# A transformer block on one core: W2 in 512 columns, the second norm by tile, and a new order of the instructions

## The chip, the core and the metric

The kernel runs on one NeuronCore of a Trainium2 chip. Its engines run side by side and meet through semaphores: TensorE (PE; its weight loads are shown as PEld), VectorE (DVE), ScalarE (ACT), GpSimd (POOL) and SyncE (SP), which here issues nearly all DMAs. The metric is device time in microseconds (us), the median of several executions; lower is better.

## What is computed

A block with adaptive layer norm: attention with 32 query heads and one shared key and value head, and a gated FFN. The input x has 2048 tokens of 1024 channels, all in bfloat16.

```
mod = silu(c) @ w_mod, split into sa, ca, ga, sb, cb, gb     (1024 each)
h = layernorm(x) * (1 + ca) + sa
q = h @ wq (32 heads of 32);  k = h @ wk;  v = h @ wv       (one head of 32)
x = x + ga * (concat_heads(softmax(q k^T / sqrt(32)) v) @ wo)
h = layernorm(x) * (1 + cb) + sb
out = x + gb * ((silu(h @ w1) * (h @ w3)) @ w2)             (F = 3584)
```

## The kernel before

**Tiling.** `build` cuts the tokens into 8 blocks n of 256 tokens, each of two tiles t of 128. An attention unit u = 8n + f is one block and four heads. A unit has 8 cycles; one cycle (`s_exp`) is 8 score matmuls of 32 rows (four at a time side by side in the array) into PSUM, and two exponentials of 128x1024 on ScalarE into one of 10 buffers U. That is 512 cycles and 1024 exponentials. Scores rotate through six PSUM banks (S); everything else on TensorE shares two banks (PB) until the last exponential has been done, and then has all eight.

**After a unit's exponentials** (`av`): VectorE adds pairs of U into PS (`pairs`) and folds these further, to 4 terms in units 2 to 7, to 1 term from unit 8 on (`level`); the denominators (`dens`) multiply the terms that are left with ones; `av_mm` makes the product with V (64 matmuls of 32 columns). In `attend` VectorE transposes the denominators, takes reciprocals, transposes back and scales, which puts the unit's output into QT. Units 0 and 1 are done together in `two_units`.

**After a block's 8 units** (`wo`): 32 matmuls of 512 columns with wo (already scaled by ga) in four sums of 8, each added to x; `ln_stats` (two BATCH_NORM_STATS2, the aggregate, then on Pool the addition of epsilon and the power −0.5) and `ln_norm` on VectorE, tile by tile. The normalised tile must be transposed for the FFN. In blocks 0 and 7, 16 PE transposes go into two banks, one for each half of the channels and each with both tiles, and VectorE applies (1 + cb) and sb out of PSUM in 8 instructions of 256 columns. In blocks 1 to 6 each tile goes through a DMA transpose into the freed part of QT, and VectorE applies the modulation there, in 8 instructions.

**FFN.** `ffn1` has 14 slabs of 256 FFN channels: 16 matmuls of 256 columns with w1, 16 with w3, a tanh on ScalarE and two VectorE instructions, which give HHT. A slab's weights (`slab_dma`, 2 x 512 KB) go into one of three buffers W13. `ffn2` has four quarters of 256 output columns (`quarter`): 28 matmuls of 256 columns for each tile, both tiles in one bank; `result` multiplies by gb and adds to x. A quarter's W2 (1792 KB) goes into one of two buffers W2S; in block 7 the last two quarters use the freed QT and U. Block n's FFN runs on TensorE during block n+1's attention. Block 7's FFN has no attention beside it.

**Order.** Every operation is a node with an engine, reads, writes, a duration and a due time (`vt`). `Placer` simulates the engines and, at each step, takes the ready node with the least due time, plus an offset for its tag and engine that `PLAN` gives. PLAN has one entry for every 8 score steps: slacks, flags and changed offsets. The engines' instruction streams are then fixed in this order. `Placer` knows a cost for each switch of TensorE between kinds of matmul (SWITCH): scores (S), AV and denominators (A), whole-array (F). Projections can also run in column form (C), in which one matmul is cut into four of 32 columns, and which needs no switch after A. `mode_of` allows column form for at most 12 operations in a row and while a running fetch load stays under FULL. Mod chunks (`mod_chunk`) compute the other parts of `mod` during block 0's attention.

All operations are emitted through `play`, so that all rows of the profile have the line 22. Rows are told apart by their tiles: `S<-QT,KT` scores, `U<-S` exponentials, `PB<-U,V` AV, `<-PS,ONES` denominators, `<-WO,QT` wo, `<-IDENT,XNB` transposes, `<-QT,W` or `<-HT,W` slabs and query projections (W is W13, whose space held wq before; the third slab buffer lies in HT, as do HHT, H20, TS and O2B), `<-W2S,HT` W2.

Of the kernel before, what the change touches and what calls it, by code (L numbers as in the profile page):

```python
# [8 lines left out]
P = 128  # L9
# [33 lines left out]
class Graph:  # L43
# [64 lines left out]
    def alias(self, new, old):  # L108
# [8 lines left out]
    (0, 0.08, 0.11, 0, 1.1, {"an/dve": 11, "av/dve": 9, "d0/sp": -38, "d1/sp": 10, "d11/sp": 2, "d12/sp": -4,  # L117
     "d2/sp": 51, "d3/sp": -151, "d6/sp": 67, "d7/sp": 32, "d8/sp": -29, "ev/act": -21, "k/pe": -26, "k/dve": 40,
     "ln/pe": -51, "ln/act": 32, "ln/dve": -11, "ln/pool": 57, "mc/pe": 52, "mc/sp": -2, "mod/pe": -62,
     "mod/dve": 10, "nm/act": 79, "pair/dve": -129, "q/pe": 3, "q/dve": -57, "quarter/pe": 11, "quarter/dve": -2,  # L120
     "s/pe": 67, "s/act": -3, "slab/pe": -5, "slab/act": 81, "slab/dve": 30, "v/pe": -8, "wo/pe": -78, "wo/dve": 1,
     "wo/sp": 36}),
    (0, 0.36, 0.11, 1, 1, {"an/dve": 8, "av/pe": -111, "av/dve": 2, "d0/sp": -31, "d1/sp": 16, "d10/sp": -66,
     "d12/sp": 63, "d13/sp": -1, "d3/sp": -14, "d5/sp": 2, "d7/sp": 84, "d8/sp": -2, "ev/act": -29, "k/pe": -36,
     "k/dve": -9, "kb/pe": 72, "ln/dve": 124, "mod/dve": -5, "nm/act": 32, "pair/dve": -104, "quarter/dve": 2,
     "s/pe": 55, "s/act": 107, "slab/pe": -26, "slab/act": -5, "slab/dve": 33, "slab/sp": 94, "v/dve": -118,
     "v/pool": -34, "wo/pe": -76, "wo/dve": 4, "wo/pool": -59, "wo/sp": 21, "d11/sp": 0, "d2/sp": 0, "d6/sp": 0,
     "ln/pe": 0, "ln/act": 0, "ln/pool": 0, "mc/pe": 0, "mc/sp": 0, "mod/pe": 0, "q/pe": 0, "q/dve": 0,
     "quarter/pe": 0, "v/pe": 0}),
    (0, 0.14, 0.18, 2, 2.9, {"q/dve": -32, "wo/dve": -44, "slab/act": 0}),  # L130
    (0.06, 0.11, 0.27, 0, 3.9, {"av/dve": 9, "d0/sp": -58, "d1/sp": 20, "d10/sp": 257, "d13/sp": 2, "d2/sp": 3,
     "d3/sp": -2, "d4/sp": 1, "d8/sp": 83, "ev/act": -11, "k/pe": -49, "k/dve": 1, "kb/dve": -7, "ln/pe": -5,
     "mc/pe": 63, "mc/sp": 5, "nm/act": 30, "out/sp": 1, "s/act": 114, "slab/sp": 4, "v/dve": 3, "v/pool": -26,
     "wo/pe": -78, "wo/dve": 14, "wo/pool": -23, "an/dve": 0, "d12/sp": 0, "d7/sp": 0, "ln/dve": 0, "mod/dve": 0,
     "pair/dve": 0, "q/dve": 0, "quarter/dve": 0, "s/pe": 0, "slab/pe": 0, "slab/dve": 0, "wo/sp": 0, "av/pe": 0,
     "d5/sp": 0, "kb/pe": 0}),
    (0, 0.11, 0.05, 0, 0.6, {"d6/sp": 19, "ev/act": -9, "k/pe": -81, "wo/pool": 7, "s/act": 0}),
    (0, 0.11, 0.05, 0, 0.6, {}),
    (0.13, 0.12, 0.23, 0, 0.7, {"av/pe": -5, "d0/sp": -4, "d10/sp": -68, "d3/sp": -46, "d9/sp": 72, "ev/act": -16,
     "kb/pe": 2, "ln/dve": -11, "mc/pe": -7, "mod/dve": -3, "q/dve": -85, "q/sp": -6, "quarter/pe": 4,  # L140
     "slab/act": 82, "slab/dve": 33, "slab/sp": 16, "wo/pe": -5, "wo/dve": 3, "wo/pool": 15, "av/dve": 0,
     "d1/sp": 0, "d2/sp": 0, "d6/sp": 0, "k/pe": 0, "k/dve": 0, "ln/pe": 0, "mc/sp": 0, "nm/act": 0, "d13/sp": 0,
     "v/dve": 0, "v/pool": 0, "d4/sp": 0, "kb/dve": 0, "out/sp": 0}),
    (0.24, 0.09, 0.2, 1, 1.4, {"av/pe": -4, "d7/sp": 78, "ev/act": -13, "ln/pool": -2, "mod/pe": 5,
     "pair/dve": -16, "slab/act": 83, "d0/sp": 0, "mod/dve": 0}),
    (0.24, 0.09, 0.02, 1, 0.4, {"d2/sp": -4}),
# [1220 lines left out]
```

## Time and profile before

| | |
|---|---|
| median of 3 runs | 1139.53 us (1138.42 to 1140.11) |
| the profiled execution | 1139.48 us |
| its span, first to last instruction | 1137.5 us |
| mean granted TensorE clock | 0.992 |
| PE / PEld busy | 1102.1 / 752.4 us |
| DVE / ACT / POOL busy | 989.8 / 1020.1 / 39.1 us |
| DMA | 209.64 MB, mean 184 GB/s |

Times in the profile count from the start of the span. A timeline row has start, length, engine, line, operation, what it writes and reads, shapes and the number of merged instructions; in brackets stands the idle time of the engine before it and what ended that. A row of a group has the busy time and the mean length in ns of one instruction, then the idle time before them and its releasers. The length of a matmul includes its way through the array; matmuls overlap, so that what one costs is the distance of their starts. "issue" as a releaser means that the engine waited for nothing that the profile shows. The granted clock is the share of full speed that TensorE got.

### The profile page before, as it was taken

Reading aid. Unit: us, or ns where it says so; the run is one execution under the profiler, and the core shown is the slowest. Engines: PE = TensorE matmul, PEld = TensorE weight load, DVE = VectorE, ACT = ScalarE, POOL = GpSimd, SP = SyncE. Lnnn points to the kernel's source line nnn. Section 1 sums busy time; section 2 is a strip of 40 time slices with the busy share of each in tenths; the row PEclk is TensorE's granted clock in tenths of the full one; section 3 lists DMA queues with packets and bytes.
Section 4 is the critical chain, followed back from the end, with each engine's and each line's share of the span. In section 5 each row is a group of like instructions: output and inputs, shape, how many; then the busy total and the mean of one; then the engine's idle time right before and its main releaser. Section 6 shows DMA issues by size and latency. Waiting matters only on the chain.

```text
span 1137.5 us, 37371 instructions
## 1 busy us (share of the span) xinstructions
PE 1102.1 (97%) x16835; PEld 752.4 (66%) x16860; DVE 989.8 (87%) x1617; ACT 1020.1 (90%) x1159; POOL 39.1 (3%) x91
## 2 busy tenths in 40 slices
PE   5999998999899999999999999999999999999998
PEld 4744536766467766777577766776567757776887
DVE  7998999999989989998999899998989899997442
ACT  5999999999999999999999999999989999994110
POOL 5200000000000000000000000000000000000000
PEclk9999989999999999999999999999999999999999
DMA  9320586675756666865596577868686558767993
GB/s 347 104 76 22 166 217 187 193 205 139 168 150 194 190 176 160 240 190 151 137 287 192 151 190 202 227 193 216 142 245 192 156 152 226 210 198 197 239 240 103
DMA packets 381535, 209.64 MB, mean 184 GB/s; under 512 B 17600, under 2 KB 373184, under 8 KB 381376
## 3 DMA queue, kind: packets, MB, share of 16 engines
q1 hardware_dynamic: 380944, 207.11, 65.9%
q8 instruction: 133, 2.18, 0.8%
q14 instruction: 26, 0.21, 0.1%
q10 hardware_dynamic: 432, 0.13, 0.0%
HBM read 199.89 MB, written 4.19 MB: 179 GB/s over the span
## 4 chain that ended last, share of the span: by engine, by line
PE 48%; ACT 42%; DVE 6%; DMA 1%; issue 1%; SPq 1%; POOL 0%; DVEq 0%
ACT U L22 39%; PE PB L22 34%; PE S L22 14%; ACT HT L22 3%; DVE PS L22 2%; DMA W<-in_A_wq_dram 1%; DVE ST L22 1%; SPq L22 1%; DVE X L22 1%; DVE RB L22 0%; DVE QT L22 0%; DVE HT L22 0%; DVE XNB L22 0%; DVE WO L22 0%; DVE MV L22 0%
## 5 line engine op out<-in xcount | busy, mean ns | idle before, releaser
L22 ACT ACTIVATE U<-S 128x1024 bf16<-128x1024 f32 x1024 | 966.6, 1142 | 11.5 <-PE S L22 10.7
L22 DVE TENSOR_TENSOR PS<-U 128x2048 bf16<-128x2048 bf16 x256 | 308.2, 1216 | 12.0 <-ACT U L22 10.1
L22 DVE TENSOR_TENSOR PS<-PS 128x1024 bf16<-128x1024 bf16 (+1 forms) x420 | 282.5, 689 | 2.5
L22 PE MATMUL PB<-QT,W 128*128 128x256 bf16 (+1 forms) x2688 | 228.1, 276 | 0.4 <-DVE HT L22 0.4
L22 PE MATMUL S<-QT,KT 32*128 32x256 bf16 x4096 | 204.7, 274 | 10.1 <-ACT U L22 7.8
L22 PEld LDWEIGHTS PB<-QT,W 128*128 128x128 bf16 (+1 forms) x2688 | 171.2, 98 | 42.0 <-issue 23.6
L22 PE MATMUL PB<-W2S,HT 128*128 128x256 bf16 x1512 | 189.3, 273 | 0.0
L22 PEld LDWEIGHTS PB<-W2S,HT 128*128 128x128 bf16 x1512 | 137.4, 98 | 41.5 <-issue 22.0
L22 PEld LDWEIGHTS S<-QT,KT 32*128 32x128 bf16 x4096 | 60.8, 92 | 139.5 <-ACT U L22 130.9
L22 PE MATMUL PB<-U,V 128*32 128x256 bf16 x4096 | 130.9, 276 | 3.5 <-issue 2.3
L22 PEld LDWEIGHTS PB<-U,V 128*32 128x32 bf16 x4096 | 101.8, 97 | 27.8 <-issue 15.3
L22 PE MATMUL PB<-QT,HT 128*128 128x256 bf16 (+1 forms) x1216 | 117.0, 273 | 0.0
L22 PE MATMUL PB<-HT,W 128*32 128x512 bf16 (+2 forms) x884 | 99.2, 343 | 3.1 <-DVE XNB L22 1.0
L22 PEld LDWEIGHTS PB<-QT,HT 128*128 128x128 bf16 (+1 forms) x1216 | 86.4, 97 | 21.0 <-issue 11.4
L22 ACT ACTIVATE HT<-PB 128x512 bf16<-128x512 f32 (+1 forms) x105 | 77.0, 733 | 7.9 <-PE PB L22 7.8
L22 DVE SCALAR_TENSOR_TENSOR HT<-HT,PB 128x512 bf16<-128x512 bf16 x100 | 68.3, 683 | 6.7 <-ACT HT L22 6.5
L22 PEld LDWEIGHTS PB<-HT,W 128*128 128x128 bf16 (+1 forms) x896 | 50.6, 97 | 34.3 <-issue 13.4
L22 DVE TENSOR_TENSOR HT<-HT,PB 128x512 bf16<-128x512 bf16 x100 | 68.2, 682 | 4.4 <-PE PB L22 3.1
L22 ACT ACTIVATE HT<-S 128x512 bf16<-128x512 f32 (+1 forms) x17 | 12.1, 721 | 58.9 <-PE S L22 58.9
L22 DVE STREAM_TRANSPOSE RB<-PB 128x256 f32<-128x256 f32 x63 | 28.0, 444 | 33.8 <-PE PB L22 33.4
L22 PE MATMUL PB<-WO,QT 128*128 128x512 bf16 (+1 forms) x260 | 53.2, 381 | 1.4 <-issue 0.6
L22 POOL TENSOR_SCALAR RS<-MV 128x1 f32<-128x1 f32 x32 | 10.2, 322 | 1009.3 <-DVE MV L22 1008.6
(111 smaller groups left out, 661.7 us busy)
## 6 DMA issues: line engine op xcount, KB each, us to landing
W<-in_B_w_dram SPq DMA_DIRECT2D x150, 512.0 KB, 4.6
W2S<-in_B_w_dram SPq DMA_DIRECT2D x30, 1792.0 KB, 8.5
HT<-in_B_w_dram SPq DMA_DIRECT2D x74, 512.0 KB, 4.7
W2S<-in_w_mod_dram SPq DMA_DIRECT2D x8, 1024.0 KB, 6.3
X<-in_A_x_dram SPq DMA_DIRECT2D x8, 512.0 KB, 7.2
U<-in_w_mod_dram SPq DMA_DIRECT2D x4, 1024.0 KB, 12.2
out_dram<-X SPq DMA_DIRECT2D x7, 512.0 KB, 7.7
W2S<-in_A_x_dram SPq DMA_DIRECT2D x5, 512.0 KB, 9.7
```

The lines of the kernel that those rows point to most:

```text
L22: return getattr(e, call[0])(*call[1], **call[2])
```

## The change

- **W2 of 512 columns.** `half` takes the place of `quarter`: two halves of 512 output columns, 28 matmuls of 512 columns for each tile, each tile in a bank of its own. A half's W2 comes in four transfers of 896 KB (7 of the 28 row blocks each) into four places. The second tile runs through the places backwards, and the next half's first part goes into the place that comes free first. In the last half of block 7, the second tile is cut into two times 256 columns.
- **Second norm by tile for blocks 0, 1 and 7.** One bank and 8 PE transposes for each tile, 16 modulations of 128 columns; block 1 no longer uses DMA transposes. In block 7 the second tile's 8 modulations run on ScalarE. In these blocks the epsilon is added on VectorE.
- **Last unit of blocks 0, 1 and 7** (`av_sharp`): the denominators take two folded terms of the first six cycles and the four half-buffers U of the last two cycles directly; AV of the first six cycles no longer waits for the last exponentials.
- **Order.** The fetch load is gone. `Placer.fetched` counts TensorE's instructions in blocks of 256 and models when a block has been fetched and when TensorE stops for one. The cap on column form by FULL goes; a switch from C to S costs 0.09 more, one from S 0.122 in place of 0.11. All of PLAN is new and longer.
- **Last block.** The sums with wo may take a bank before all that they read is ready (after the last exponential). Slabs 3 to 5 go into three places in the freed U.
- **Smaller ones.** The bias of query groups 2 to 7 is computed in four column groups at once (`q_bias_rest`); the scaled wq has keys of its own; the diagonal for the gate rows lies in W2's space and not in a norm buffer; mod chunks are due at 4 + 3i in place of 8 + 5i. `act_stats` is defined but used by no tile.

The core of the diff:

```diff
-    SWITCH = {"F": 0.095, "S": 0.11, "A": 0.106, "C": 0.106}
+    SWITCH = {"F": 0.095, "S": 0.122, "A": 0.106, "C": 0.106}
+    CS = 0.09
-    FULL = 36.0
-    FETCH = 24.0
+    BLOCK, AHEAD, STOP, CALL, MOST, LAND = 256, 141, 430, 0.6, 4.5, 2.6
...
-        return n.col[1][0] or ("C" if self.mode in ("A", "C") and self.ncol < self.COLS and self.load < self.FULL else "F")
+        return n.col[1][0] or ("C" if self.mode in ("A", "C") and self.ncol < self.COLS else "F")
...
+    def fetched(self, count):
+        self.pos += 2 * count
+        while self.pos >= self.BLOCK * len(self.fetch) + self.AHEAD:
+            self.fetch.append(min(max(self.t["pe"] + self.CALL, self.bw), self.t["pe"] + self.CALL + self.MOST) + self.LAND)
+        while self.pos >= self.BLOCK * self.got + self.STOP:
+            self.t["pe"] = max(self.t["pe"], self.fetch[self.got])
+            self.got += 1
...
+    def av_sharp(u):
+        s = Sess(False)
+        c0 = u * NJ
+        for q in range(0, NP - 2, 2):
+            pairs(c0 + q)
+        G.tag = "av"
+        fold(c0 + 2, 0, 2)
...
+        for q in range(NJ):
+            av_mm(u, c0 + q, q, s, q == 0, q == NJ - 1, [exps[(c0 + (5 if q < 6 else 7), 1)]])
+        sd = Sess()
+        terms = [("U", c0 + q, kk) for q in (6, 7) for kk in range(2)]
+        terms = [("PS", 0, 0), ("PS", 4, 0)] + terms
...
-                s = Sess()
+                s = Sess(n < NB - 1)
...
+                       after=[exps[(64 * NB - 1, 1)]] if n == NB - 1 else ())
...
-            if 0 < n < NB - 1:
+            if 1 < n < NB - 1:
...
-        for hh in range(2):
+        for t in range(2):
             s = Sess()
+            op("pe", lambda b, t=t: [lambda e, cc=cc: e.transpose(
+                BANKH[b][:, cc * P:(cc + 1) * P], XN[t][:, cc * P:(cc + 1) * P], IDENT[:]) for cc in range(NC)], 0.5,
+               reads=[("XN", t), "IDENT"], writes=[("h2", n, t)], vt=vt, mode="F", sess=s, post=0.145)
...
+    W13U = [Uf[:, (2 + k) * 4096:(3 + k) * 4096].rearrange("p (m c f) -> p m c f", m=2, c=NC) for k in range(3)]
...
+        if n == NB - 1 and 3 <= s < 6:
+            return W13U[s - 3], ("W13U", s - 3)
...
-    def quarter(n, q, vt):
+    def half(n, h, vt0, vt1):
         G.tag = "quarter"
+        for k in range(4):
+            w2_dma(n, h, k, vt0 + k - (200 if n == NB - 1 and h and k < 2 else 20))
+        ends = n == NB - 1 and h == 1
+        for t in range(2):
+            vt = vt0 + (vt1 - vt0) * t / 2
+            parts = [(0, 256), (256, 512)] if ends and t else [(0, 512)]
+            order = [(k, i) for k in (range(4) if t == 0 else range(3, -1, -1)) for i in range(NK)]
...
-        mod_chunk(i, 8.0 + 5 * i)
+        mod_chunk(i, 4.0 + 3 * i)
...
-            av(8 * n + f)
+            (av_sharp if f == NC - 1 and n in (0, 1, NB - 1) else av)(8 * n + f)
         e0 = 64.0 * (n + 1)
-        wo(n, e0 - 30)
+        wo(n, e0 - (330 if n == NB - 1 else 30))
```

568 lines of the change are left out of this document (347 added, 221 removed), and 10 rows, old and new, of the table PLAN.

## The prediction

> **What bounds the kernel now.** I read the page's chain first, then the busy times by stretch, then the timeline of the stretches in which TensorE stands idle.
>
> ```profile
> span 1137.5 us, 37371 instructions
> PE 48%; ACT 42%; DVE 6%; DMA 1%; issue 1%; SPq 1%; POOL 0%; DVEq 0%
> L22 ACT ACTIVATE U<-S 128x1024 bf16<-128x1024 f32 x1024 | 966.6, 1142 | 11.5 <-PE S L22 10.7
> ```
>
> The chain is shared by TensorE and ScalarE. ScalarE's 1024 exponentials take 966.6 us, and it stood idle for only 11.5 us ahead of them. The windows view (stretch; its length, then busy time of PE, PEld, DVE, ACT, POOL; clock; DMA share; GB/s) shows which of the two sets the end:
>
> ```profile
> 31.00:147.00 116.00, 112.82 (x2120) 60.72 (x2128) 107.11 (x187) 115.55 (x126) 7.24 (x17) 1.00 0.26 87
> 147.00:190.00 43.00, 37.96 (x567) 19.92 (x572) 39.09 (x70) 39.75 (x45) 2.44 (x4) 0.93 0.82 222
> 303.00:319.00 16.00, 10.13 (x171) 4.67 (x164) 14.05 (x29) 14.85 (x17) 0.79 (x2) 0.79 0.63 134
> 319.00:829.00 510.00, 507.66 (x7939) 349.50 (x7949) 470.18 (x746) 507.67 (x581) 7.43 (x16) 1.00 0.71 191
> 829.00:842.00 13.00, 10.48 (x220) 6.84 (x214) 9.37 (x15) 9.56 (x13) 0.00 (x0) 0.87 0.85 230
> 842.00:1038.00 196.00, 195.51 (x3037) 136.87 (x3032) 181.25 (x286) 194.78 (x224) 2.44 (x4) 1.00 0.68 187
> 1038.00:1060.50 22.50, 22.45 (x231) 16.70 (x230) 15.93 (x34) 0.05 (x1) 1.69 (x4) 1.00 0.95 244
> 1060.50:1135.00 74.50, 74.19 (x680) 66.24 (x678) 24.95 (x41) 8.36 (x14) 0.00 (x0) 1.00 0.75 199
> ```
>
> From 319 us on, TensorE works without a break to 1135 us, except for one hole at 829 to 842 us. Both engines are full in between, and after 1038 us (the last exponential) TensorE works alone. So the end is TensorE's work, plus the time it lost earlier. It lost time in three places: 147 to 190 (5.0 us idle and a clock of 0.93), 303 to 319 (5.9 us idle, clock 0.79) and 829 to 842 (2.5 us idle, clock 0.87). Time won there is work done before 1038 us that is not left over behind it. Idle time before 147 us doesn't count in the same way: ScalarE is full there, and TensorE has little else to do until block 0's attention is complete.
>
> **Part A, block 1's second norm by PE transposes.**
>
> ```profile
> 283.56 1.06 PE L22 MATMUL PB<-U,V 128*32 128x256 bf16 x32
> 308.58 0.55 DVE L22 TENSOR_SCALAR XNB<-X,MV,RS 128x1024 bf16<-128x1024 bf16 x1
> 308.81 0.40 PE L22 MATMUL S<-QT,KT 32*128 32x256 bf16 x8 [1.44 <-ACT U L22]
> 309.16 1.24 SPq L22 DMA_TRANSPOSE QT<-XNB  x1
> 311.55 1.90 PE L22 MATMUL PB<-U,V 128*32 128x256 bf16 x32 [0.30 <-ACT U L22]
> 313.93 1.90 PE L22 MATMUL PB<-U,V 128*32 128x256 bf16 x32
> 316.22 2.13 DVE L22 TENSOR_SCALAR QT<-QT,MODC 128x256 bf16<-128x256 bf16 x8
> 317.83 1.70 PE L22 MATMUL PB<-QT,HT 128*128 128x256 bf16 x14
> ```
>
> The second tile is normalised at 309.13. Its transpose goes through a DMA, the modulation follows at 316.22, and the first slab at 317.83, which is 8.7 us later. Meanwhile block 0's FFN has run out, and TensorE has only scores and AV, in the end at half speed (twice 32 AV matmuls in 1.90 us, against 1.06). After the change come 8 transposes for each tile and 16 modulations out of PSUM. Block 0 does this today in other sizes:
>
> ```profile
> 157.21 1.06 PE L22 MATMUL PB<-U,V 128*32 128x256 bf16 x32
> 159.60 0.80 PE L22 MATMUL PB<-PS,ONES 128*32 128x256 bf16 x16
> 174.01 0.55 DVE L22 TENSOR_SCALAR XNB<-X,MV,RS 128x1024 bf16<-128x1024 bf16 x1 [0.77 <-POOL RS L22]
> 174.61 1.07 PE L22 MATMUL PB<-IDENT,XNB 128*128 128x128 bf16 x16 [0.47 <-DVE XNB L22]
> 175.40 2.64 DVE L22 TENSOR_SCALAR HT<-PB,MODC 128x256 bf16<-128x256 bf16 x8
> 176.91 0.94 PE L22 MATMUL PB<-HT,W 128*128 128x256 bf16 x6 [0.90 <-DVE HT L22]
> ```
>
> From the end of the second norm (174.56) to the first slab matmul (176.91) it took 2.35 us. Block 1's slab would start 8.7 − 2.35 = 6.35 us earlier. The hole's loss caps that: 5.9 us of idle time and 0.21 × 16 = 3.4 us of clock, 9.3 in all, less 1.07 us for the 16 new transposes, 8.2. The gain is 6.35, and I take **−6**. Bounds: −8.2 and −2. The last holds if the modulations are slow: 16 of them, each between 0.19 us (the 128x128 row below, 3.0 us for 16) and 0.33 us (2.64 for 8 of twice the width), are 3.0 to 5.3 us on a VectorE that is nearly full, and they hold both free PSUM banks so long. Behind them on VectorE queue the pair sums, for which the denominators of the next unit wait.
>
> ```profile
> L22 DVE TENSOR_SCALAR XNB<-IDENT,MG 128x128 bf16<-128x128 bf16 x16 | 3.0, 249 | 0.1
> ```
>
> **Part B, block 0's norm by tile, and the last unit's sums.** In block 0 the first tile's transposes and modulations move ahead of the second tile's norm, so only 8 modulations stand behind it. That is half of 2.64 us, −1.3. The epsilon step moves from Pool to VectorE and saves a part of the 0.77 us for which the norm waited. The last unit of blocks 0 and 1 now sums four of its six denominator terms directly from U: at 159.60 the denominators waited for the last folds, though AV had been done at 158.27. That is −1.3 where the chain is open, and there it is open. TensorE pays 24 matmuls in place of 16 (block 0) or 4 (blocks 1 and 7). At 0.11 us for four (32 AV matmuls take 1.06, of which 0.27 is the length of the last) that is 0.22 + 0.55 + 0.55 = +1.3. I take **−3 and +1.3**. Bounds: the whole loss of the stretch, 5.0 idle and 0.07 × 43 = 3.0 of clock, −8; and 0 if the order puts other work in that gap. The projections of later blocks, the mod chunks (due earlier now, every 3 instead of 5 steps), the query bias in column form and the diagonal's new place all lie before 160 us, where ScalarE is the bound. They cost 0; if they slip behind 160 us, they are filler for this same gap.
>
> **Part C, order planned with fetches.**
>
> ```profile
> 324.18 1.48 PE L22 MATMUL PB<-QT,W 128*32 128x256 bf16 x48
> 834.55 0.29 PE L22 MATMUL PB<-U,V 128*32 128x256 bf16 x4 [2.33 <-issue]
> 835.33 2.56 PE L22 MATMUL PB<-QT,W 128*32 128x256 bf16 x48
> q8 instruction: 133, 2.18, 0.8%
> ```
>
> In the middle of a run of 64 AV matmuls TensorE stood for 2.33 us with nothing to wait for in the profile, and the next 48 column matmuls ran 1.08 us slower than the same 48 at 324.18. By the window, the hole costs 2.5 us of idle time and 0.13 × 13 = 1.7 us of clock, 4.2. The page shows 133 instruction loads of 16 KB. A late one, in a dense run of short instructions, is the likeliest reading of a stop without a releaser. The new planner counts instructions in blocks of 256 and no longer caps the column form by a fetch load. Bounds: −4.2 (hole gone) and 0 (it stays, or comes elsewhere). I take **−2**. [...]
>
> The retuned offsets move nearly every instruction. From 319 to 1038 us TensorE has nothing to win apart from that hole (its busy time is 99.5% and 99.8% of the two stretches), so a new order can only lose there. Bounds 0 to +5 (one hole like 829 to 842, rounded up). I take **+2**.
>
> **Part D, W2 of 512 columns.**
>
> ```profile
> 1045.72 6.85 PE L22 MATMUL S<-WO,QT 128*128 128x512 bf16 x31
> 1110.08 6.28 PE L22 MATMUL S<-W2S,HT 128*128 128x256 bf16 x56
> L22 PE MATMUL S<-WO,QT 128*128 128x512 bf16 x31 | 6.9, 379 | 0.1
> L22 PE MATMUL PB<-W2S,HT 128*128 128x256 bf16 x1512 | 189.3, 273 | 0.0
> ```
>
> Less the length of the last one (379 and 273 ns), a 512-column matmul follows the one before after (6.85 − 0.38)/30 = 0.2157 us, one of 256 columns after (6.28 − 0.27)/55 = 0.1093 us. Two of the narrow ones cost 2.9 ns more than a wide one. The 1792 narrow ones become 868 wide ones and 56 narrow: 868 × 2.9 ns = **−2.5**. The bounds are 0 and −2.5. Weight loads halve too, but the narrow matmuls already hide them (0.1093 is matmul time). VectorE does as many results as before, of the same size. SP issues eight transfers per block in place of four; nothing near waits for W2 in before, so 0.
>
> **Part E, the last block.**
>
> ```profile
> 1021.27 16.79 ACT L22 ACTIVATE U<-S 128x1024 bf16<-128x1024 f32 x18 [0.56 <-PE S L22]
> 1038.94 1.93 PE L22 MATMUL PB<-U,V 128*32 128x256 bf16 x64
> 1043.74 0.29 PE L22 MATMUL S<-PS,ONES 128*32 128x256 bf16 x4
> 1045.29 0.42 DVE L22 TENSOR_TENSOR QT<-RB 128x256 bf16<-128x256 f32 x1
> 1060.51 3.66 PE L22 MATMUL S<-QT,HT 128*128 128x256 bf16 x32
> 1135.19 0.29 DVE L22 TENSOR_TENSOR X<-X,HT 128x256 bf16<-128x256 bf16 x1
> ```
>
> From the last exponential (1038.06) to the first slab (1060.51) go 22.45 us, but TensorE fills them all: AV 1.9, wo 6.9, transposes 1.1 as in block 0, and left-over W2 matmuls of block 6 for the other 12 us or so. Shortening this chain (sums ahead, direct denominators, half of the modulations on an idle ScalarE) thus gains **0** by itself. It is the room that A to D need: when they take 10 us from the left-over work, the chain must fit into 22.4 − 10 = 12 us, plus what the last exponential comes earlier. My estimate of the chain, from these rows: 1.5 us for the last AV and denominator matmuls; 2.0 from there to QT (1043.74 to 1045.71); and then the 14.8 us from QT to the slab less three quarters of wo, 5.1, now summed before. That is 13.2 us. ScalarE stands idle for 3.2 + 1.2 + 3.4 us in the holes of A to C, and half of that makes the room. What is over is lost again. The new wait of wo for the last exponential holds up what stands behind it on TensorE, W2 filler; the AV ahead of it waits for the same exponential. Three slabs in U move 3 MB into the time after AV; no weight is late now (TensorE is busy for 74.19 of the last 74.50 us), so 0.
>
> **Sum.** −6 − 3 + 1.3 − 2 + 2 − 2.5 = −10.2 us. The profiled execution took 1139.48 us (span 1137.5 and 2.0 around it), the median of the three runs is 1139.53; so 1139.5 − 10.2 = 1129 us.
>
> **Rivals.**
> - *All of it comes back*: A −8.2, B −8 + 1.3, C −4.2, D −2.5, nothing lost to the order: −21.6, or 1118 us. ScalarE must then also lose all of its 11.5 us of idle time: 1038.06 − 11.5 + 13.2 + 74.5 + 2.5 + 2.0 = 1119 us, which is the floor. For it: the idle times of both engines stand in the same three holes. Against: a new order that has no hole at all.
> - *The hole isn't a fetch* (the mechanism of part C falls): −8.2, 1131 us.
> - *Banks and VectorE eat the gain*: the 16 modulations take 5.3 us in block 1 and hold both banks. A gives −2, B 0 + 1.3, C 0, the order +2, D −2.5: −1.2, 1138 us, within the noise of a measurement. VectorE's 88% in 303 to 319 speaks for it, block 0's 2.35 us against it.
> - *Slower, by holes in the instruction stream*: column-form runs behind AV runs (64 + 96 matmuls and as many loads) come without the old cap. If they stop TensorE as at 832 us, each stop costs 4.2 us. The gain without C and the order is 10.2, so three new stops use it up; with five it is 1139.5 − 10.2 + 21 = 1150 us. For it: the one hole came in just such a run. Against: many such runs passed without one.
>
> **Chances.** Forecast 0.52, no fetch 0.10, all of it 0.14, banks 0.08, slower 0.16. The likeliest case by itself spans 1123 to 1135 (A and B at half or in full). The range leaves out the slower case and a little of the best one: 1117 to 1140. About 0.2% (2.3 us) is what a measurement of this kernel can tell from no change. Faster by more than that: 0.52 + 0.10 + 0.14 and a quarter of the banks case, 0.78; within it 0.06; slower 0.16.
>
> **What would show it.** A: between block 1's wo and its first slab, no idle TensorE and a clock near 1.00. B: the same for 147 to 190 us. C: no "issue" gap over 1 us within a run of short matmuls. D: the W2 group with half the count and 0.2157 us apart. E: TensorE without idle time between the last exponential and the first slab, and that distance at 13 to 17 us, down from 22.45. Idle time there means that the chain sets the end; new idle time between 319 and 1038 us, or several issue gaps, means that the order failed; an unchanged 300 to 320 us means that the third rival holds.

## The result, and the profile after

The changed kernel takes **1140.59 us** (median of 9 runs, 1139.32 to 1142.25), against 1138.34 us for the kernel before in the same session (9 runs): a ratio of **1.0025, interval 1.0013 to 1.0037**. It is slower by a quarter of a per cent, 2 to 3 us (1.5 to 4.2 by the interval), where 1129 us were forecast, and it lies just above the range. Five lines of the page of the changed kernel: its span, the chain's shares, ScalarE's exponentials, the wide W2 matmuls and the instruction loads.

```profile
span 1138.7 us, 32824 instructions
PE 59%; ACT 31%; DVE 7%; POOL 2%; issue 1%; DMA 1%; SPq 0%
L22 ACT ACTIVATE U<-S 128x1024 bf16<-128x1024 f32 x1024 | 965.7, 1144 | 13.7 <-PE S L22 10.6
L22 PE MATMUL PB<-W2S,HT 128*128 128x512 bf16 x756 | 190.2, 381 | 0.6 <-DVE X L22 0.6
q8 instruction: 114, 1.87, 0.7%
```

The windows view of the changed kernel (columns as in the prediction: length, then busy time of PE, PEld, DVE, ACT, POOL; clock; DMA share; GB/s), over the same stretches:

```profile
31.00:147.00 116.00, 113.17 (x1768) 59.56 (x1766) 107.64 (x185) 113.57 (x125) 5.57 (x16) 1.00 0.25 83
147.00:190.00 43.00, 39.41 (x548) 20.53 (x548) 39.20 (x84) 41.37 (x47) 2.00 (x2) 0.96 0.79 230
303.00:319.00 16.00, 13.90 (x206) 9.28 (x205) 15.62 (x35) 14.92 (x17) 0.00 (x0) 1.00 0.80 250
319.00:829.00 510.00, 505.05 (x6645) 297.75 (x6643) 469.03 (x744) 506.79 (x578) 12.67 (x16) 1.00 0.65 190
829.00:842.00 13.00, 13.00 (x244) 9.88 (x236) 12.59 (x20) 11.62 (x15) 0.00 (x0) 1.00 0.94 266
842.00:1008.00 166.00, 164.50 (x2183) 101.81 (x2182) 151.69 (x236) 163.70 (x189) 3.10 (x4) 1.00 0.65 188
1008.00:1038.00 30.00, 29.94 (x368) 15.68 (x364) 25.79 (x42) 25.08 (x29) 0.00 (x0) 1.00 0.56 169
1060.50:1135.00 74.50, 73.55 (x599) 57.50 (x598) 26.35 (x46) 11.28 (x22) 0.00 (x0) 1.00 0.59 169
```

The prediction had taken the stretch from 842 to 1038 us as one. Cut at 1008, the kernel before had:

```profile
842.00:1008.00 166.00, 165.57 (x2544) 114.78 (x2542) 153.51 (x244) 165.41 (x192) 2.44 (x4) 1.00 0.70 191
1008.00:1038.00 30.00, 29.94 (x505) 22.08 (x494) 27.73 (x43) 29.37 (x34) 0.00 (x0) 1.00 0.58 161
```

Read TensorE's column first: the holes shrank. At 303 to 319 us it is busy for 13.90 us instead of 10.13, and the clock is 1.00 instead of 0.79; at 829 to 842 us 13.00 instead of 10.48; at 147 to 190 us, where the hole did not close, 39.41 instead of 37.96 (clock 0.96 instead of 0.93). Now read ScalarE's column, the fourth. At 303 to 319 us it stays where it was (14.85, now 14.92), and at 1008 to 1038 us it *loses* 4.3 us (29.37, now 25.08). The end of each block's last exponential, from the traces, says the same:

| block | 0 | 1 | 2 | 3 | 4 | 5 | 6 | 7 |
|---|---|---|---|---|---|---|---|---|
| before, us | 154.69 | 282.10 | 408.41 | 533.50 | 658.45 | 783.73 | 912.69 | 1038.05 |
| changed, us | 155.89 | 282.10 | 408.43 | 532.69 | 659.14 | 785.75 | 913.68 | 1045.21 |

After both early holes (the norms of blocks 0 and 1) ScalarE stands where it stood, and it ends 7.2 us later. Put as a sum along ScalarE and then along the tail (each from the gaps between instructions in the traces):

| us | before | changed |
|---|---|---|
| first exponential starts | 30.8 | 30.4 |
| exponentials, net of overlap | 942.4 | 942.4 |
| tanh and other ScalarE work up to the last exponential | 53.1 | 54.2 |
| ScalarE idle up to there | 11.8 | 18.1 |
| last exponential to first slab matmul | 22.45 | 17.25 |
| first slab to last matmul, and the rest | 77.0 | 76.2 |

The tail got 6.0 us shorter (−5.2 and −0.8), and ScalarE's idle time and work took 7.4 us more. Of the idle time, 5.7 us lie after 1000 us (0.6 before). The profiled execution of the kernel before (1139.48 us) lies 1.1 us above that kernel's median here, so the two traces show less of the difference than the medians do.

### The profile page after: what moved, and what is told of

Read it like the earlier page. It is cut to its first block, busy times and chain, and to the rows that moved or that the text cites. A ratio compares the mean times of both kernels' runs of the same rounds, so it can differ in the third digit from the quotient of the medians.

```text
span 1138.7 us, 32824 instructions
## 1 busy us (share of the span) xinstructions
PE 1109.4 (97%) x14545; PEld 666.4 (59%) x14545; DVE 988.9 (87%) x1628; ACT 1025.1 (90%) x1167; POOL 41.5 (4%) x85
## 4 chain that ended last, share of the span: by engine, by line
PE 59%; ACT 31%; DVE 7%; POOL 2%; issue 1%; DMA 1%; SPq 0%
PE PB L22 44%; ACT U L22 28%; PE S L22 15%; ACT HT L22 2%; DVE PS L22 2%; POOL RS L22 1%; DVE ST L22 1%; DVE X L22 1%; DVE QT L22 1%; DVE HT L22 1%; DMA U<-in_w_mod_dram 1%; DVE XNB L22 0%; POOL WO L22 0%; DVE RB L22 0%; DVE MV L22 0%
## 5 line engine op out<-in xcount | busy, mean ns | idle before, releaser
L22 PEld LDWEIGHTS PB<-QT,W 128*128 128x128 bf16 (+1 forms) x1888 | 167.9, 98 | 48.2 <-issue 23.2
L22 PE MATMUL PB<-W2S,HT 128*128 128x512 bf16 x756 | 190.2, 381 | 0.6 <-DVE X L22 0.6
L22 PE MATMUL PB<-U,V 128*32 128x256 bf16 x4096 | 126.8, 273 | 1.3 <-ACT U L22 1.3
L22 PE MATMUL PB<-QT,HT 128*128 128x256 bf16 (+1 forms) x956 | 122.2, 275 | 1.7 <-ACT QT L22 0.9
L22 PEld LDWEIGHTS PB<-W2S,HT 128*128 128x128 bf16 x756 | 63.1, 97 | 85.3 <-issue 25.2
L22 PEld LDWEIGHTS PB<-QT,HT 128*128 128x128 bf16 x956 | 87.6, 98 | 27.4 <-issue 13.6
L22 PE MATMUL PB<-HT,W 128*128 128x256 bf16 (+1 forms) x560 | 100.9, 323 | 0.6 <-DVE HT L22 0.3
L22 PEld LDWEIGHTS PB<-HT,W 128*128 128x128 bf16 x560 | 49.4, 98 | 36.7 <-issue 11.6
L22 PE MATMUL PB<-WO,QT 128*128 128x512 bf16 x224 | 56.3, 380 | 0.3 <-DVE RB L22 0.3
L22 DVE COPY RB<-PB 128x256 f32<-128x256 f32 x62 | 26.1, 420 | 11.0 <-PE PB L22 10.3
```

The lines of the kernel that those rows point to most:

```text
L22: return getattr(e, call[0])(*call[1], **call[2])
```

## The experiments

**Theories.** The prediction's premise: from 319 us on TensorE's work sets the end, so time that it wins anywhere counts. *Theory 1*: up to about 1008 us ScalarE sets the pace, and only what ScalarE wins counts. *Theory 2*: in the last stretch TensorE does, from 913 us on. *Theory 3*, formed after theory 2 fell: TensorE does from about 1008 us on, and the changes to the last block trade time ahead of the last exponential for time behind it.

Ratios to the kernel before, each measured in the same session as its run; the changed kernel is 1.0025, from a session of its own. One thousandth is 1.14 us. A difference between two of these ratios is uncertain by about 2 us, so small ones are read together with the traces.

| run | based on | ratio | interval |
|---|---|---|---|
| pe_mid | changed | 1.0024 | 1.0009 to 1.0039 |
| act_mid | changed | 0.9989 | 0.9974 to 1.0004 |
| both_mid | changed | 0.9979 | 0.9968 to 0.9990 |
| b_pe_mid | before | 0.9999 | 0.9985 to 1.0014 |
| b_act_mid | before | 0.9961 | 0.9945 to 0.9977 |
| pe_late | changed | 1.0022 | 1.0008 to 1.0036 |
| act_late | changed | 1.0006 | 0.9993 to 1.0018 |
| b_shift | before | 0.9995 | 0.9983 to 1.0008 |
| b_nohole | before | 1.0000 | 0.9986 to 1.0013 |
| pe_end | changed | 1.0055 | 1.0036 to 1.0074 |
| pe_end2 | changed | 1.0012 | 1.0002 to 1.0023 |
| scores_first | changed | 1.0020 | 1.0005 to 1.0035 |
| e_none | changed | 1.0086 | 1.0063 to 1.0110 |
| b_last | before | 1.0010 | 0.9998 to 1.0021 |
| d_split | changed | 1.0037 | 1.0026 to 1.0048 |

### Who sets the pace of the middle: pe_mid, act_mid, both_mid

The order of the instructions is kept, and one engine gets a little less to do in each step.

```diff
+        wd = 246 if n in (1, 2, 3, 4) else B
...
-                        lambda cc=cc: h2t(n)[:, cc, :], cc == 0, cc == NC - 1) for cc in range(c0, c0 + 2)])
+                        lambda cc=cc: h2t(n)[:, cc, 0:wd if cc else B], cc == 0, cc == NC - 1) for cc in range(c0, c0 + 2)])
```

That is pe_mid, in `slab` (the output is cut in the same way); act_mid, in `s_exp`:

```diff
+        wd = 504 if 1 < n < 6 else 512
...
-                    S6[:, 2 * r[i]:2 * r[i] + 2, :], ACT.Exp, scale=SCALE)]
+                    S6[:, 2 * r[i]:2 * r[i] + 2, 0:wd], ACT.Exp, scale=SCALE)]
```

> The changed kernel with its order kept and a little less TensorE work in the middle: in the slabs of blocks 1 to 4 (they run from 282 to about 790 us) seven of eight matmuls have 246 in place of 256 columns. That leaves a part of the FFN of these blocks out. It is 4 x 392 matmuls x 4.17 ns = 6.5 us less for TensorE, spread evenly. Theory 1 (ScalarE sets the pace of the middle: 124.6 of 125 us per block are busy, and TensorE waits for it at the block ends): 0 to 1.5 us faster than the changed kernel, and TensorE's idle time in the middle grows by about 6 us. Rival (the premise of the prediction: TensorE's work sets the end from 319 us on): 6 us faster.

> The changed kernel with its order kept and a little less ScalarE work in the middle: the exponentials of blocks 2 to 5 (282 to 786 us) take 504 of the 512 columns of each half, which leaves a part of the softmax of these blocks out. By the distance of a 512-column tanh and a 1024-column exponential (0.50 and 0.92 us) that is about 13 ns for each of 512 exponentials, 6.7 us. Theory 1 (ScalarE sets the pace of the middle): the last exponential of block 5 ends 3 to 6 us earlier (TensorE has 1 to 1.5 us per block to give), the end 3 to 5 us earlier. Rival (TensorE sets the pace): no change within 1 us.

> The changed kernel, order kept, with the cuts of pe_mid and act_mid together (a part of the FFN of blocks 1 to 4 and of the softmax of blocks 2 to 5 is left out): 6.5 us less for TensorE and 6.2 us less for ScalarE between 282 and 790 us. If the two engines run in step there, with ScalarE a little ahead as the bound, the last exponential of block 5 ends 5 to 6 us earlier and the end comes 4.5 to 6 us earlier, more than the 3.8 us of ScalarE's cut alone. If the gain of act_mid was limited by something else (the block ends, the last block), no more than 4 us.

By the distances of part D, a column of a matmul is (0.2157 − 0.1093)/256 us = 0.416 ns, and ten of them in each of 1568 matmuls make the 6.5 us. They gained nothing (1.0024). The window of pe_mid shows where they went. With it stands the window of pe_late (a run of a later section), which is uncut in this stretch:

```profile
319.00:829.00 510.00, 498.51 (x6621) 298.20 (x6645) 469.56 (x744) 507.28 (x578) 12.66 (x16) 1.00 0.66 190
319.00:829.00 510.00, 501.06 (x6617) 297.84 (x6641) 469.15 (x744) 506.79 (x578) 12.66 (x16) 1.00 0.66 190
```

The window of act_mid shows what ScalarE's cut does:

```profile
319.00:829.00 510.00, 502.19 (x6664) 301.52 (x6696) 472.05 (x752) 505.29 (x584) 12.66 (x16) 1.00 0.67 192
```

In pe_mid TensorE's busy time is 498.51 us against 505.05 in the changed kernel, but that is not the size of the cut's effect: the traces of pe_mid, act_mid, pe_late and act_late hold 14467 matmuls for 14545 weight loads, so that 78 matmul records are missing, 31 of them wide ones (512 columns) of this stretch. With the same records missing and no cut here, pe_late has 501.06 us. So the cut shows as 2.5 us more idle time, not the 6 that were expected, and ScalarE stays at 507 of 510: no time was won. In act_mid ScalarE and VectorE get through more in the same 510 us, 584 and 752 instructions instead of 578 and 744. It is 0.36% faster than the changed kernel, 4.1 us of the 6.2 by which its exponentials got shorter in the trace. With both cuts it is 0.46%, 5.2 us. The traces agree: from block 1's last exponential to block 5's go 503.7 us in the changed kernel, 502.9 in pe_mid, 499.2 in act_mid and 498.1 in both_mid. So ScalarE sets the pace, with TensorE close behind it: by the traces its cut is worth about 1 us once ScalarE's is made, which the times alone can't tell from nothing. Theory 1 holds for the middle, and the premise does not.

### The same on the kernel before: b_pe_mid, b_act_mid

The same two edits.

> The kernel before with its order kept and the same cut as in pe_mid: seven of eight slab matmuls of blocks 1 to 4 have 246 columns, which leaves a part of the FFN of these blocks out; 6.5 us less for TensorE between 282 and 790 us. If ScalarE paces the middle of the kernel before too (its idle time from 330 to 800 us is about 2 us), nothing is gained: 0 to 1.5 us. Rival (the premise of the prediction, read off this very kernel: TensorE's work sets the end from 319 us on): 5 to 6 us faster.

> The kernel before with its order kept and the same cut as in act_mid: the exponentials of blocks 2 to 5 take 504 of the 512 columns of each half, which leaves a part of their softmax out; that made 6.2 us less for ScalarE there. If both engines are full in the middle of this kernel, ScalarE's time alone gains less than in the changed kernel, because TensorE has only 0.3 to 0.5 us of idle time per 100 us: 1 to 2.5 us. If ScalarE alone paces it: 3.5 to 5 us. If TensorE alone does: 0 to 0.5 us.

0.9999 and 0.9961: nothing for TensorE's cut, 4.4 us for ScalarE's. The answer lay in the kernel that I had read. What had misled me is TensorE's busy time. These are the windows of b_pe_mid and of b_last, a run of a later section that is uncut here:

```profile
319.00:829.00 510.00, 506.14 (x7954) 349.46 (x7955) 470.52 (x745) 507.16 (x580) 7.43 (x16) 1.00 0.71 191
319.00:829.00 510.00, 508.51 (x7966) 349.68 (x7958) 470.20 (x746) 507.67 (x580) 7.43 (x16) 1.00 0.71 192
```

With 6.5 us less to do, TensorE is busy for only 2.4 us less than in b_last. (The 507.66 us of the kernel before are a little low: 25 matmul records are missing from its trace, none from these two.) A matmul of 256 columns is 273 ns long in the profile, and the next one starts 109 ns later, so a wait of a tenth of a microsecond between two starts doesn't show as idle: 99.5% busy is not full. My expectation for b_act_mid had made the same mistake and was too low (1 to 2.5 us).

### Was the hole at 303 us worth anything: b_nohole

```diff
         for p, strong in sorted(n.preds.items(), key=lambda a: -a[0].i):
+            if n in self.loose and p in self.free:
+                continue
...
-                dma("sp", h2t(n)[:, :, t * P:(t + 1) * P], XN[t], ("H2", t), 1 << 18, reads=[("XN", t)],
-                    writes=[("H2R", n, t)], vt=vt - 40, bw=100e3, transpose=True)
+                free.append(dma("sp", *((FREE[:, t], XN[t][:, 0:P]) if n == 1 else (h2t(n)[:, :, t * P:(t + 1) * P], XN[t])), ("H2", t), 1 << 18, reads=[("XN", t)],
+                    writes=[("H2R", n, t)], vt=vt - 40, bw=100e3, **({"transpose": True} if n > 1 else {})))
```

`loose` holds block 1's eight modulations, `free` its two DMAs.

> The kernel before, order kept, with the wait for block 1's DMA transposes taken out: the modulations of block 1 work on what lies in their place already, and the two transposes become copies of 128 columns to a place of their own. That leaves block 1's second transpose out. The hole at 303 to 319 us (5.9 us of TensorE idle, 1.15 us of ScalarE idle) should nearly close: block 1's first slab comes 4 to 6 us earlier. By the prediction's part A (time won there is work that is not left over at the end): 4 to 6 us faster than before. By theory 1 (only what ScalarE wins counts): 0 to 1 us faster, with block 2's last exponential within 1 us of 408.4.

The time is unchanged (1.0000), but the experiment missed its aim: the hole did not close. VectorE's rows of b_nohole, with the modulations last:

```profile
312.43 1.28 DVE L22 TENSOR_TENSOR PS<-PS 128x1024 bf16<-128x1024 bf16 x2
315.52 0.42 DVE L22 COPY RB<-PB 128x256 f32<-128x256 f32 x1 [1.81 <-PE PB L22]
315.87 2.13 DVE L22 TENSOR_SCALAR QT<-QT,MODC 128x256 bf16<-128x256 bf16 x8
```

The modulations come 0.35 us earlier, not 5, and so does all the rest of this run there (its block 1 ended at 281.74 us, 0.36 earlier than before). They had not been waiting for the transposes: ahead of them in VectorE's queue stands a copy that waits for an AV product, and that waits for exponentials. TensorE's rows in the hole of the kernel before say who was late:

```profile
306.97 0.40 PE L22 MATMUL S<-QT,KT 32*128 32x256 bf16 x8 [1.44 <-ACT U L22]
310.64 0.61 PE L22 MATMUL S<-QT,KT 32*128 32x256 bf16 x8 [1.44 <-ACT U L22]
317.50 0.40 PE L22 MATMUL S<-QT,KT 32*128 32x256 bf16 x8 [1.13 <-ACT U L22]
```

Every wait names the exponentials (ACT U), and 306.97, 308.81 and 310.64 are 1.83 to 1.84 us apart, the time of two exponentials (twelve run from 302.23 to 313.34 us, 0.92 us from one start to the next). TensorE had no slab to work on, and its scores waited *because ScalarE was full*. In the changed kernel the same waits stand at the block ends. TensorE's rows after block 3's attention, and then ScalarE's:

```profile
559.26 0.29 PE L22 MATMUL PB<-PS,ONES 128*32 128x256 bf16 x4 [0.70 <-DVE PS L22]
562.40 0.40 PE L22 MATMUL S<-QT,KT 32*128 32x256 bf16 x8
563.11 1.93 PE L22 MATMUL PB<-U,V 128*32 128x256 bf16 x64 [0.32 <-ACT U L22]
565.45 1.33 PE L22 MATMUL PB<-QT,W 128*128 128x256 bf16 x6
```

```profile
561.12 3.77 ACT L22 ACTIVATE U<-S 128x1024 bf16<-128x1024 f32 x4 [0.47 <-PE S L22]
565.42 2.85 ACT L22 ACTIVATE U<-S 128x1024 bf16<-128x1024 f32 x3 [0.53 <-PE S L22]
```

The W2 work of the block before has run out by 562.40 us (in the kernel before it lasted to 568), the next slab's modulations start at 564.71, and between them TensorE waits. Its lead in FFN work ends here in waits, and ScalarE, which has no wait here in the kernel before, loses about 1 us. A kernel with part A alone and an order planned for it was not tried.

### The stop at 834 us: b_shift

```diff
             @block.tensor
             def _(e):
+                product, need = self.warm
+                e.wait_ge(self.sem[need.sem], need.val)
+                for _ in range(64):
+                    play(e, self.small(REC))
...
+    pl.small = lambda e: e.matmul(BANK[5][:, 0:2], IDENT[:], IDENT[:, 0:2], start=True, stop=True)
```

> The kernel before with 64 matmuls of 2 columns ahead of all TensorE work, in a time in which TensorE waits for its first data; with their weight loads that moves all later instructions by 128 places, half of a 16 KB load. Theory (the stop of 2.33 us at 834.55 is a late load of instructions): the stop goes or moves to another place of that run; without it the end comes 2 to 4 us earlier. Rival (something else stops TensorE there): the stop stays at the same matmul, time within 1 us.

The stop moved. These are b_shift's rows:

```profile
830.89 1.93 PE L22 MATMUL PB<-U,V 128*32 128x256 bf16 x64
833.30 1.38 PE L22 MATMUL PB<-QT,W 128*32 128x256 bf16 x43
835.41 0.38 PE L22 MATMUL PB<-QT,W 128*32 128x256 bf16 x5 [0.73 <-issue]
```

In the kernel before, and in the four other runs with its TensorE stream up to there (b_pe_mid, b_act_mid, b_nohole, b_last), it stands behind the same 60th AV matmul, with 2.33, 1.42, 1.69, 0.65 and 1.96 us. One of them, b_nohole:

```profile
831.08 1.82 PE L22 MATMUL PB<-U,V 128*32 128x256 bf16 x60
833.56 0.29 PE L22 MATMUL PB<-U,V 128*32 128x256 bf16 x4 [0.65 <-issue]
```

So it belongs to a place in the instruction stream. The page of the kernel before has 133 instruction loads of 16 KB for 33695 matmuls and weight loads, one for 253 of them, so that the 128 places of b_shift are about half of one. The DMA records name the load: in each of these six executions a 16 KB transfer of the instruction queue landed shortly before TensorE went on (in the kernel before it ran from 831.89 to 833.07 us, in b_shift from 833.00 to 834.08). From its landing to the end of the stop it took 1.3 to 1.5 us each time, however long the stop was. That fits a late load, as the prediction had it, and in the kernel before it is the only one: after 30 us TensorE has six gaps of over 1 us there, and this one alone (2.33 us) has no releaser. Its length is different in each execution, the one profiled before had the longest, and with b_shift the time did not change (0.9995).

### The last stretch: pe_late, act_late

The edits of pe_mid and act_mid with other values:

```diff
+        wd = 238 if n in (6,) else B
...
+        wd = 498 if n == 7 else 512
```

> The changed kernel with its order kept and less TensorE work beside block 7's attention alone: in the slabs of block 6 seven of eight matmuls have 238 in place of 256 columns, which leaves a part of the FFN of that block out; 392 x 7.5 ns = 2.9 us less. Theory 2 (in the last stretch, from 913 us on, TensorE sets the pace and ScalarE waits for it): 2.5 to 3 us faster than the changed kernel, the last exponential earlier by the same. Rival (ScalarE sets the pace there too): 0 to 0.5 us.

> The changed kernel with its order kept and less ScalarE work in block 7 alone: its exponentials take 498 of the 512 columns of each half, which leaves a part of the softmax of that block out; about 23 ns for each of 128 exponentials, 2.9 us. Theory 2 (TensorE sets the pace of the last stretch): 0 to 0.5 us faster than the changed kernel, and ScalarE's idle time after 913 us grows by 2.5 us or more. Rival (ScalarE sets the pace): 2.5 to 3 us faster.

1.0022 and 1.0006: 0.3 us for TensorE's cut, 2.2 us for ScalarE's. The second is loose: by their medians (1140.37 and 1139.90 us, same session) the two runs are only 0.5 us apart. In the traces block 7's exponentials end 131.53 us after block 6's in the changed kernel, 131.17 in pe_late and 130.31 in act_late, and ScalarE's idle time after 913 us grew by 1.0 us in act_late, not by 2.5. So ScalarE's cut gained something and TensorE's next to nothing, the reverse of what theory 2 expected. Between 842 and 1008 us TensorE is busy in pe_late for 1.4 us less than in pe_mid, which lacks the same records and has no cut here, and ScalarE for as long as ever. First pe_late, then pe_mid:

```profile
842.00:1008.00 166.00, 161.99 (x2173) 101.84 (x2179) 151.38 (x235) 163.69 (x189) 3.10 (x4) 1.00 0.65 188
842.00:1008.00 166.00, 163.40 (x2169) 101.94 (x2177) 151.57 (x235) 163.69 (x189) 3.09 (x4) 1.00 0.66 188
```

Theory 2 fell. But ScalarE's idle time after 1000 us stayed in both runs (5.4 and 6.2 us). The changed kernel there, TensorE's rows and then ScalarE's:

```profile
1012.45 0.40 PE L22 MATMUL S<-QT,KT 32*128 32x256 bf16 x8
1012.78 0.29 PE L22 MATMUL PB<-PS,ONES 128*32 128x256 bf16 x4
1013.01 3.01 PE L22 MATMUL PB<-QT,W 128*128 128x256 bf16 x26
1015.95 1.93 PE L22 MATMUL PB<-U,V 128*32 128x256 bf16 x64
1017.81 0.39 PE L22 MATMUL PB<-W2S,HT 128*128 128x512 bf16 x1
1018.13 0.40 PE L22 MATMUL S<-QT,KT 32*128 32x256 bf16 x8
```

```profile
1010.21 2.85 ACT L22 ACTIVATE U<-S 128x1024 bf16<-128x1024 f32 x3
1014.31 0.60 ACT L22 ACTIVATE HT<-PB 128x512 bf16<-128x512 f32 x1 [1.24 <-PE PB L22]
1016.86 6.52 ACT L22 ACTIVATE U<-S 128x1024 bf16<-128x1024 f32 x7 [1.95 <-PE PB L22]
```

Between the scores at 1012.45 and at 1018.13 TensorE does 5.3 us of other work without a break, and ScalarE waits for it. What TensorE's time is worth here, the next runs ask.

### From 1008 us on: pe_end, pe_end2, scores_first

```diff
+                    e1 = c1 - 64 if n == 6 and (k, i) != order[0] else c1
...
-                           BANK[b][:, c0:c1], HHT[:, f, t * P:(t + 1) * P], w2[:, i, c0:c1], start=first, stop=last)],
+                           BANK[b][:, c0:e1], HHT[:, f, t * P:(t + 1) * P], w2[:, i, c0:e1], start=first, stop=last)],
```

That is pe_end2, in `half`; scores_first has other values in the last 8 entries of PLAN (`PLAN[57:65]`) and nothing else.

> The changed kernel, order kept, with less TensorE work from 1014 to 1060 us alone: all but the first matmul of each W2 sum of block 6 have 448 in place of 512 columns, which leaves a part of that block's result out; 108 x 26.7 ns = 2.9 us. Theory 3 (from about 1008 us on TensorE sets the pace: ScalarE waits 5.7 us there, for scores that stand behind TensorE's FFN work): 2.5 to 3 us faster than the changed kernel. Rival (ScalarE or the chain behind the last exponential sets the end): 0 to 0.7 us.

> The changed kernel, order kept, with all but the first matmul of each W2 sum of block 6 at 448 in place of 512 columns (a part of that block's result is left out) and block 7 as it was; 108 x 26.7 ns = 2.9 us less for TensorE between 1014 and 1060 us. In pe_end the edit had also widened the 28 matmuls of block 7's last sum but one from 256 to 512 columns, 3.0 us more at the very end, so that its 3.3 us on top of the changed kernel say little. Theory 3 (TensorE sets the pace from 1008 us on): 2 to 3 us faster than the changed kernel. Rival (the chain from the last exponential to the first slab, with ScalarE's exponentials ahead of it, sets the end): 0 to 1 us.

> The changed kernel with another order of block 7's second half alone (the last 8 of the 65 entries of PLAN): scores come earlier against the FFN work of block 6, of which more is left for the time after the last exponential. Nothing is left out. Theory 3 (TensorE sets the end from 1008 us on, ScalarE's 5.7 us of idle time there are a consequence): the last exponential ends 2 to 4 us earlier, the end stays within 1 us. Rival (the idle time of ScalarE after 1000 us is what makes the changed kernel late): 2 to 4 us faster.

pe_end was a faulty edit, as the expectation of pe_end2 says: it also made 28 matmuls at the very end twice as wide. pe_end2 is 0.13% faster than the changed kernel, 1.5 of 2.9 us: between the two theories. Its trace has 0.3 us more idle TensorE than the changed kernel at 1038 to 1060.5 us:

```profile
1038.00:1060.50 22.50, 22.14 (x205) 10.65 (x202) 15.96 (x29) 7.94 (x9) 1.09 (x2) 1.00 1.05 301
```

(22.46 there in the changed kernel.) In the changed kernel TensorE already waits a little for the chain:

```profile
1060.90 0.61 PE L22 MATMUL S<-IDENT,XNB 128*128 128x128 bf16 x8
1062.46 0.38 PE L22 MATMUL PB<-QT,HT 128*128 128x256 bf16 x2 [0.95 <-ACT QT L22]
```

In scores_first the last exponential comes 3.0 us earlier (1042.22), and the time is the same within the interval (1.0020). ScalarE's late idle time is thus mostly a consequence: what isn't done ahead of the last scores is done behind them. Of pe_end2's 2.9 us, its trace shows 0.4 won up to the last exponential (131.12 us after block 6's, 131.53 in the changed kernel) and 1.0 behind it (16.20 us to the first slab instead of 17.24). So theory 3 holds in part: TensorE's time counts there, but only about half of it.

### The last block's changes: e_none, b_last

```diff
-                s = Sess(n < NB - 1)
+                s = Sess()
...
-                if t and n == NB - 1:
+                if False:
...
-        if n == NB - 1 and 3 <= s < 6:
-            return W13U[s - 3], ("W13U", s - 3)
-        r = (n * NSLAB + s - (3 if n == NB - 1 and s > 5 else 0)) % NW
+        r = (n * NSLAB + s) % NW
...
-            (av_sharp if f == NC - 1 and n in (0, 1, NB - 1) else av)(8 * n + f)
+            (av_sharp if f == NC - 1 and n in (0, 1) else av)(8 * n + f)
...
-        wo(n, e0 - (330 if n == NB - 1 else 30))
+        wo(n, e0 - 30)
```

That is e_none, on the changed kernel; b_last puts the same pieces, and block 7's norm by tile, into the kernel before, with other values in `PLAN[57:65]`.

> The changed kernel without its changes to the last block: the last unit by the plain folds, wo's sums only when all that they read is there and due as in the other blocks, all 16 modulations on VectorE, slabs 3 to 5 in the ordinary three places. The norm by tile and W2 stay. The order up to about 1030 us is that of the changed kernel. The prediction gave these changes 0 by themselves: then the end stays within 1.5 us, though the distance from the last exponential to the first slab grows by some us. If they carry a gain that the rest has lost: 3 to 5 us slower.

> The kernel before with the changes to the last block alone (last unit's sums from U, wo summed when its bank is free, norm by tile with half of the modulations on ScalarE, slabs 3 to 5 in U), and the order of block 7's second half planned for them (the last 8 entries of PLAN). The prediction gave this part 0 by itself. Theory 3 (a trade: less W2 work is left to fill the shorter chain, so more of it stands ahead of the last scores): the last exponential 4 to 6 us later than before, the way from there to the first slab 4 to 6 us shorter, the end within 1.5 us of before. Rival (the shorter chain is a gain that the other parts lost): 4 to 5 us faster than before.

b_last is the trade itself: ratio 1.0010, last exponential at 1042.27 (4.2 us later; 5.3 us, counted from block 6's), first slab 16.6 us behind it instead of 22.45. The last run of exponentials on ScalarE, and the first slab on TensorE:

```profile
1018.28 23.99 ACT L22 ACTIVATE U<-S 128x1024 bf16<-128x1024 f32 x26 [1.64 <-PE S L22]
```

```profile
1058.86 1.36 PE L22 MATMUL S<-QT,HT 128*128 128x256 bf16 x11
```

A shorter chain needs less W2 work to fill it, so that work moves ahead of the last scores, where ScalarE waits for it: in b_last it is idle for 5.8 us after 1000 us, as in the changed kernel (5.7), against 0.6 before. In the changed kernel the part can't be missed all the same: e_none (4 runs) is 0.61% (7 us) slower, because with the little W2 that its order leaves, the old chain is open: its first slab comes 23.5 us after its last exponential, not 17.25. Its TensorE:

```profile
1062.15 0.62 PE L22 MATMUL PB<-IDENT,XNB 128*128 128x128 bf16 x8 [1.24 <-DVE XNB L22]
1065.69 1.03 PE L22 MATMUL PB<-IDENT,XNB 128*128 128x128 bf16 x8 [2.92 <-DVE XNB L22]
1067.50 2.72 PE L22 MATMUL S<-QT,HT 128*128 128x256 bf16 x12 [0.78 <-DVE QT L22]
```

The expectation (within 1.5 us, if the part is worth nothing by itself) failed for this base: what is worth 0 in one order is a support of another.

### W2 as two of 256: d_split

```diff
-                       last=(k, i) == order[-1]: [lambda e: e.matmul(
-                           BANK[b][:, c0:c1], HHT[:, f, t * P:(t + 1) * P], w2[:, i, c0:c1], start=first, stop=last)],
+                       last=(k, i) == order[-1]: [lambda e, y=y: e.matmul(
+                           BANK[b][:, y:y + 256], HHT[:, f, t * P:(t + 1) * P], w2[:, i, y:y + 256], start=first,
+                           stop=last, skip_group_check=True) for y in range(c0, c1, 256)],
```

> The changed kernel, order kept, with each W2 matmul of 512 columns issued as two of 256 (the work is the same): 868 more matmuls, 868 x 2.9 ns = 2.5 us more for TensorE and 868 weight loads more. By the prediction's term D: 2.5 us slower. Theory 1 with theory 3 (TensorE's time counts only after about 1008 us): only block 6's and block 7's W2 count, 196 x 2.9 ns = 0.6 us slower, not to be told from no change.

(This run also leaves out the call of `Placer.fetched`; its trace has TensorE's groups in the order of the changed kernel.) 1.0037: 1.4 us slower than the changed kernel, between the two expectations (0.6 and 2.5) and, with both intervals, not told from either.

## Why the prediction was wrong

**The step that failed** stands under "What bounds the kernel now": "So the end is TensorE's work, plus the time it lost earlier", and then "Time won there is work done before 1038 us that is not left over behind it." In its place the runs showed that ScalarE paces the middle: between 282 and 790 us TensorE's cut of 6.5 us is worth nothing in either kernel, ScalarE's of about 6 us is worth 4. From there to about 1008 us the evidence is thinner (pe_late and act_late, 0.3 and 0.5 to 2.2 us of 2.9), and behind that TensorE's time counts in part. The rows under part A had the sign of it: the waits in the hole at 303 us name ACT U.

- **A** (−6): the mechanism worked, most of the hole is closed (2.1 us idle instead of 5.9), the clock is 1.00. Its worth was wrong. ScalarE had lost only 1.15 us there, and won 0.07. That A is worth next to nothing is argued from this and from the cuts; no run had A alone.
- **B** (−3 and +1.3): the hole closed in part (3.6 us idle instead of 5.0, clock 0.96). ScalarE won 1.6 us at 147 to 190 (39.75 to 41.37) and was busy 2.0 us less ahead of it (115.55 to 113.57). By 282.10 us both profiled executions are level.
- **C** (−2): a late load by the DMA records (its stop ends 1.3 to 1.5 us after a landing), as argued, and gone; no "issue" gap of the changed kernel's weight loads is over 1.1 us. But the sum was made against an execution with the longest stop seen, and in b_shift, where the stop of 0.73 us stands elsewhere, the time did not change. What a kernel before without any stop would take was not measured.
- **D** (−2.5): one wide matmul per 0.2157 us was forecast; the 28 at 1054.41 us (6.21 us long) give (6.21 − 0.38)/27 = 0.216. By the cuts, little of it can count ahead of 1008 us; d_split does not settle its worth.
- **E** (0): right, by b_last. The chain was put too short: 13.2 us were estimated, but the distance is 17.25 us with 0.95 us of wait for the second tile's modulations, and 16.2 in pe_end2, which has less W2 to fill it.
- **The order** (+2): mis-sized, and put in the wrong place. I had said that a new order can only lose between 319 and 1038 us, and it did: ScalarE's idle time after 500 us rose from 6.5 to 12.6 us, of which 5.1 us after 1000 us is the trade with the tail.

The slower rival did not come about: no new stop in the instruction stream (after 30 us TensorE has no gap of over 1 us). The banks rival came close in time (1138 us) by luck, not by its mechanism: the hole at 303 us mostly closed, and the 16 modulations took 2 x 2.11 us. "All of it comes back" had noted that ScalarE must then lose all of its idle time. That sentence, taken as the bound of each part and not of that rival alone, would have cut A to 1.2 us: ScalarE's idle time in the three holes was 3.2 + 1.2 + 3.4 us. It would still have left room for a small gain.

## What to carry to other kernels

Where two engines both look full, value a hole by what the *pacing* engine loses in it, and find that engine from the releasers of the waits inside the hole: here the waits for ACT in TensorE's hole (1.44 us each at 306.97, 308.81 and 310.64) went with a stretch in which 6.5 us of TensorE's time were worth nothing (0.9999). A small even cut of one engine's work, with the order kept, measures what its time is worth, and it can be done on the kernel before. Compare the counts of matmuls and of weight loads before you compare TensorE's busy time in two traces: the traces with 14467 matmuls for 14545 loads lacked records, and showed idle time that wasn't there (in pe_late 501.06 us busy where the changed kernel has 505.05). A shorter chain at the end of a pipeline is a gain only if the work that used to fill it has somewhere free to go: in b_last it went from 22.45 to 16.6 us, at a ratio of 1.0010.

## What the runs showed of the hardware

- A stop of TensorE without a releaser stood at the same instruction in five executions and was 0.65 to 2.33 us long; 64 matmuls more ahead of it moved it by 47 matmuls. In all six it ended 1.3 to 1.5 us after a 16 KB instruction load had landed.
- TensorE's busy time in the profile fell by about 2.5 us when 6.5 us of matmul columns were taken out of some 510 us, in both orders (b_pe_mid against b_last 2.4, pe_mid against pe_late 2.5): the share of busy time didn't measure the slack.
- 16 of 1024 columns less made an exponential 12 ns shorter (942.4 to 936.2 us over 512 of them).
